# Lightning attention followed by a GELU MLP: a rebuilt prologue, an undecayed state and a last tile in two parts

## The chip, the cores and the metric

One core of one Trainium2 chip runs the whole kernel. The metric is the device time of one execution, in microseconds (us). The kernel before was timed three times: 237.8 us median, 237.49 to 241.02.

## The reference

Block-wise linear attention with a decay per head, then a two-layer MLP with a GELU. Batch 4, 8 heads, 768 positions, head size 64, blocks of 64; the MLP goes from 512 to 2048 and back, over 3072 tokens.

```python
Dmask = np.where(rel >= 0, lam[:, None, None] ** rel[None, :, :], 0.0)
...
for b in range(nb):
    intra = np.einsum('bhic,bhjc->bhij', qb, kb) * Dmask[None]
    intra = np.einsum('bhij,bhjd->bhid', intra, vb)
    inter = np.einsum('bhid,bhde->bhie', qb * lam_pow[None], kv_state)
    out[:, :, sl] = intra + inter
    kb_dec = kb * rev_pow[None]
    kv_state = lam_block[None, :, None, None] * kv_state + np.einsum('bhsd,bhse->bhde', kb_dec, vb)
...
h = x @ w_in
g = 0.5 * h * (1.0 + np.tanh(c * (h + 0.044715 * h * h * h)))
return (g @ w_out).astype(np.float32)
```

## The kernel before, in words

The kernel works in blocks of 128 positions, two of them (index c) to a superblock of 256 (`SB`). There are 24 steps; step s takes one superblock of one batch and one half of the heads (four heads, two pairs `hp` of two heads `hl`). Three superblocks make a sequence, so every six steps the state starts anew.

The decay is put on q and v: q is multiplied by lam to the power of a position (`dq`), v by the reciprocal (`dv`), and the scores are then only masked with ones and zeros (`mask`). Between blocks of 128 the state is multiplied by lam to the power 128.

A step goes through these functions:

- `load_step` (L60) issues three DMAs of 256 KB on the SyncE queue, for q, k and v. `load_win` and `load_wout` (L76, L82) bring the weights in eight pieces of 1 MB into a ring of four buffers (`wst`), `cast_win` and `cast_wout` (L88, L100) turn them into 16 bits: the first piece of w_in on ScalarE, the other three on VectorE, w_out on GpSimd.
- `prep` (L164) makes 16-bit q, k, v: q times `dq` on VectorE (L177), k on ScalarE (L178), v times `dv` on GpSimd (L179).
- `stage_t` (L184) transposes q and k on TensorE into one PSUM tile `Tps` (eight 128x128 transposes, L190) and copies it to `qkT` (L193, VectorE).
- `region(n, s)` (L205) issues for step n the scores `Sps` (16 matmuls, L223), the state's increment K into a part of the tile `OK` (L234), and the masking of the scores to `PT` on VectorE (L240); and for the step s before it the output matmuls (L255) and those with the state (L265), which ScalarE copies to `xT` (L272). There is one buffer each of `Tps`, `Sps` and `OK`.
- `update(n, c)` (L279) adds K to the state on VectorE (`t`, L292 and L294), and GpSimd multiplies the sum with lam^128 twice: into `u` for the next addition (L299) and, head by head, into the block-diagonal 16-bit `ubd` that TensorE uses as weights (L302, two instructions). `t` of the next block reads `u`.

The MLP of a group of superblocks is cut into pieces of work in a list, `filler`: `mm1` (first layer and GELU on ScalarE) and `mm2` (a quarter of a 128-token output tile; after the fourth quarter VectorE copies the tile to `o32` and SyncE writes it with two DMAs, L343 and L345). `fill(n)` takes n pieces from that list. The order of all instructions is the program's order on each engine (`pin`), written out by hand: steps 0 to 3 first (the prologue, L374 to L391), then the weights' casts and `fill(19)`, steps 4 to 7 with their own `fill` counts (L398 to L423), and a loop for the rest. TensorE, VectorE, ScalarE, GpSimd and SyncE each go through their own part of that order without overtaking.

The constants are made at the start, mostly on GpSimd (L126 to L159): `dq` by a power of 16 columns (L132), a power of 8 columns for lam^128 (L149), and eight cleared `ubd` tiles (L159).

Of the kernel before, what the change touches and what calls it, by code (L numbers as in the profile page):

```python
# [15 lines left out]
def kernel(  # L16
# [10 lines left out]
    nc = tc.nc  # L27
# [105 lines left out]
    dv = const.tile([P, H, 2], FP32)
    nc.vector.reciprocal(dv[:], dq[:])
    ident = const.tile([P, P], FP16)
    make_identity(nc, ident)
# [4 lines left out]
    nc.gpsimd.tensor_scalar(rel[64:128], rel[64:128], 128.0, None, ALU.add)  # L141
    mask = const.tile([P, 2 * P], FP32)
    nc.vector.tensor_scalar(mask[:], rel[:].rearrange("p a b c -> p (a b c)"), 0.0, None,
                            ALU.is_ge)

    p128 = const.tile([P, H], FP32)
    nc.gpsimd.memset(p128[:], 128.0)
    lam128 = const.tile([P, H], FP32)
    nc.gpsimd.tensor_tensor(lam128[:], lam_bc[:], p128[:], ALU.pow)  # L149
    lamu = const.tile([P, H // 2], FP32)  # L150
    l3 = lam128[:].rearrange("p (hp two) -> p hp two", two=2)
    nc.gpsimd.tensor_copy(out=lamu[0:64, :], in_=l3[0:64, :, 0])
    nc.gpsimd.tensor_copy(out=lamu[64:128, :], in_=l3[64:128, :, 1])

    ubd = [[const.tile([P, 2, P], FP16, name=f"ubd_{hf}_{i}", tag=f"ubd_{hf}_{i}")
            for i in range(4)] for hf in range(2)]
# [39 lines left out]
    PTs = {}  # L196
# [5 lines left out]
    def half64(i):  # L202
        return slice(64 * i, 64 * i + 64)

    def region(n, s):  # L205
# [54 lines left out]
        for c in range(2):  # L260
            u = ins[c]
            if u is None:
                continue
            for hp in range(2):
                pin(nc.tensor.matmul(OK[:, c, hp * P : hp * P + P], u[:, hp, :],  # L265
                                     o[:, 0, hp, :, half64(c)], start=False, stop=True,
                                     skip_group_check=True))
        g, i = group_of[sbg]
# [5 lines left out]
                                 func=AF.Copy))  # L274

    ins_of = {}
    turn = [0, 0]

    def update(s, c):  # L279

        sbg, half = divmod(s, 2)
        sb = sbg % NSB
        if c == 0:
            ins_of[s] = [state[half][1] if sb > 0 else None, None]
        if c == 1 and sb == NSB - 1:
# [9 lines left out]
        lu = lamu[:, 2 * half : 2 * half + 2].unsqueeze(2).to_broadcast([P, 2, D])  # L295
        bd = ubd[half][turn[half] % 4]
        turn[half] += 1
        uc = ucp.tile([P, 2, D], FP32, tag=f"u{half}", name=f"u_{s}_{c}")
# [13 lines left out]
    def queue_group(g):  # L312
# [158 lines left out]
```

## Time and profile before

| | us |
|---|---|
| median of three runs | 237.8 |
| the profiled execution | 237.57 |
| its span in the trace | 235.7 |
| TensorE busy (share of the span) | 208.0 (88%) |
| VectorE busy | 95.5 (41%) |
| ScalarE busy | 89.0 (38%) |
| GpSimd busy | 93.5 (40%) |
| bytes moved by DMA | 33.89 MB |

The span runs from the first to the last event of the trace; 1.87 us of the profiled execution lie outside it. PE is TensorE, PEld its weight loads, DVE VectorE, ACT ScalarE, POOL GpSimd, SP SyncE; a trailing q is an engine's issuing queue. Times inside the trace are us from the span's start.

### The profile page before, as it was taken

To read this page: it belongs to the slowest core of one execution; us is meant where nothing else is said; L and a number is where in the kernel's file an instruction comes from. 1 tells how busy PE (TensorE), PEld (TensorE's weight loads), DVE (VectorE), ACT (ScalarE), POOL (GpSimd) and SP (SyncE) were. 2 spreads that over 40 slices of the span, in tenths; PEclk is the share of its full clock that TensorE was granted. 3 is DMA by queue.
4 is the path that set the end of the run, shared out by engine and by line. 5 is a ranking of instruction groups with operands and counts; after the bars stand their busy time and mean duration, and the time that the engine had idled before them with its cause. 6 is when DMAs were issued, how large, how long until landed. Compare 5 with 4: busy or idle time off the path is not lost.

```text
span 235.7 us, 5205 instructions
## 1 busy us (share of the span) xinstructions
PE 208.0 (88%) x2192; PEld 113.1 (48%) x2192; DVE 95.5 (41%) x144; ACT 89.0 (38%) x150; POOL 93.5 (40%) x175
## 2 busy tenths in 40 slices
PE   0237599969779999999999999999999999999992
PEld 0126334435458668554545545454554544444440
DVE  0448661045667673564434534335452332100121
ACT  2204376601226417326751137621157610267000
POOL 4989885317277453353254133235325110000000
PEclk9999999999999999999999999999999999999997
DMA  5999789999637058329802739303720012300223
GB/s 150 290 351 386 240 258 323 335 292 273 141 99 218 3 155 238 104 45 243 204 3 45 190 91 302 90 0 70 204 45 0 3 41 51 76 13 3 44 56 79
DMA packets 46247, 33.89 MB, mean 144 GB/s; under 512 B 2192, under 2 KB 39056, under 8 KB 46224
## 3 DMA queue, kind: packets, MB, share of 16 engines
q1 hardware_dynamic: 46080, 33.56, 53.0%
q8 instruction: 17, 0.28, 0.5%
q14 instruction: 6, 0.05, 0.1%
q10 hardware_dynamic: 144, 0.00, 0.0%
HBM read 27.27 MB, written 6.29 MB: 142 GB/s over the span
## 4 chain that ended last, share of the span: by engine, by line
PE 87%; POOL 5%; DVE 3%; ACT 2%; issue 2%; POOLq 0%
PE Hps L324 36%; PE O2ps L335 35%; PE Tps L190 4%; PE Sps L223 4%; PE OK L265 3%; PE OK L255 3%; PE OK L234 1%; POOL dq L132 1%; POOL lam L149 1%; DVE q L177 1%; ACT w_in L92 1%; POOL ubd L159 1%; DVE o L343 1%; ACT xT L272 1%; DVE qkT L193 1%
## 5 line engine op out<-in xcount | busy, mean ns | idle before, releaser
L324 PE MATMUL Hps<-xT,w_in 128*128 128x512 f16 (+1 forms) x448 | 88.0, 352 | 0.0
L335 PE MATMUL O2ps<-w_out,gT 128*128 128x512 f16 x384 | 86.8, 379 | 0.0
L326 ACT ACTIVATE gT<-Hps 128x512 f16<-128x512 f32 x96 | 57.3, 597 | 46.1 <-PE Hps L324 46.1
L324 PEld LDWEIGHTS <-w_in 128*128 128x128 f16 x448 | 43.4, 99 | 37.2 <-issue 1.7
L335 PEld LDWEIGHTS <-gT 128*128 128x128 f16 x384 | 36.6, 98 | 40.2
L299 POOL TENSOR_TENSOR u<-t,lamu 128x128 f32<-128x128 f32 x40 | 17.0, 424 | 89.6 <-DVE t L294 63.0
L272 ACT ACTIVATE xT<-OK 128x512 f16<-128x512 f32 x24 | 14.3, 597 | 73.9 <-PE OK L265 73.9
L343 DVE COPY o<-O2ps 128x512 f32<-128x512 f32 x24 | 16.6, 690 | 54.3 <-PE O2ps L335 54.1
L240 DVE TENSOR_TENSOR PT<-Sps,mask 128x1024 f16<-128x1024 f32 x24 | 29.3, 1221 | 22.8 <-PE Sps L223 22.8
L302 POOL TENSOR_TENSOR ubd<-t,lamu 64x128 f16<-64x128 f32 x80 | 33.5, 418 | 3.0
L193 DVE COPY qkT<-Tps 128x1024 f16<-128x1024 f16 x24 | 16.5, 689 | 36.8 <-PE Tps L190 36.8
L179 POOL TENSOR_TENSOR v<-v,dv 128x512 f16<-128x512 f32 x24 | 25.3, 1055 | 2.2 <-DMA v<-in_v_dram 0.6
L190 PE MATMUL Tps<-ident,q 128*128 128x128 f16 x96 | 10.2, 235 | 14.7 <-DVE q L177 14.7
L177 DVE TENSOR_TENSOR q<-q,dq 128x512 f16<-128x512 f32 x24 | 19.8, 823 | 2.5 <-DMA q<-in_q_dram 2.5
L178 ACT ACTIVATE k<-k 128x512 f16<-128x512 f32 x24 | 14.7, 622 | 7.8 <-DMA k<-in_k_dram 7.8
L190 PEld LDWEIGHTS <-q 128*128 128x128 f16 x96 | 7.5, 105 | 19.3 <-DVE q L177 15.8
L223 PE MATMUL Sps<-qkT 64*64 64x128 f16 x384 | 10.9, 237 | 3.1 <-DVE qkT L193 3.1
L294 DVE TENSOR_TENSOR t<-OK,u 128x128 f32<-128x128 f32 x32 | 9.2, 288 | 9.0 <-POOL u L299 7.0
L255 PE MATMUL OK<-PT,v 64*64 64x128 f16 x384 | 11.1, 233 | 1.9 <-DVE t L294 1.9
L223 PEld LDWEIGHTS <-qkT 64*64 64x64 f16 x384 | 6.7, 114 | 11.8 <-issue 6.1
L234 PE MATMUL OK<-v,k 64*64 64x64 f16 x320 | 7.6, 202 | 3.4 <-POOL v L179 3.0
L103 POOL CAST w_out<-wo 128x1024 f16<-128x1024 f32 x8 | 9.1, 1169 | 3.1 <-DMA wo<-in_moe_w_out_dram 3.1
(29 smaller groups left out, 69.1 us busy)
## 6 DMA issues: line engine op xcount, KB each, us to landing
q<-in_q_dram SPq DMA_DIRECT2D x24, 256.0 KB, 5.4
k<-in_k_dram SPq DMA_DIRECT2D x24, 256.0 KB, 5.3
v<-in_v_dram SPq DMA_DIRECT2D x24, 256.0 KB, 5.2
out_dram<-o SPq DMA_DIRECT2D x48, 128.0 KB, 2.4
wi<-in_moe_w_in_dram SPq DMA_DIRECT2D x4, 1024.0 KB, 10.5
wo<-in_moe_w_out_dram SPq DMA_DIRECT2D x4, 1024.0 KB, 7.8
lam_bc<-in_lam_dram ACTq DMA_DIRECT2D x1, 4.0 KB, 3.6
```

The source lines that it names most:

```text
L177: pin(nc.vector.tensor_tensor(wide(tq), q32[:], decay(dq), ALU.mult))
L179: pin(nc.gpsimd.tensor_tensor(wide(tv), v32[:], decay(dv), ALU.mult))
L190: pin(nc.tensor.transpose(Tps[:, i, hp, j, :], t[:, j, 2 * hp : 2 * hp + 2, :], ident[:]))
L193: pin(nc.vector.tensor_copy(out=o[:], in_=Tps[:]))
L223: pin(nc.tensor.matmul(Sps[half64(c), hl, hp, jk, :], o[half64(hl), 1, hp, jk, half64(c)], o[half64(hl), 0, hp, :, half64(c)], start=True, ...
L240: pin(nc.vector.tensor_tensor(PT[:].rearrange("p a b c d -> p (a b) (c d)"), Sps[:].rearrange("p a b c d -> p (a b) (c d)"), mask[:].unsqu ...
L255: pin(nc.tensor.matmul(OK[half64(hl), c, hp * P : hp * P + P], tv[half64(c), jk, 2 * hp + hl, :], PT[half64(c), hl, hp, jk, :], start=star ...
L302: pin(nc.gpsimd.tensor_tensor(bd[r, :, half64(hl)], t[r], lu[r], ALU.mult))
L324: pin(nc.tensor.matmul(Hps[:, i, :], w_in16[:, c, f * P : (f + 1) * P], x[:, c, :], start=(c == 0), stop=(c == NC - 1)))
L326: pin(nc.scalar.activation(out=gT[:, f0 : f0 + per, :], in_=Hps[:], func=AF.Gelu_apprx_tanh))
L335: pin(nc.tensor.matmul(O2[tau][:], gT[:, f, tau * P : (tau + 1) * P], w_out16[:, f, :], start=(f == 0), stop=(f == NF - 1)))
L343: pin(nc.vector.tensor_copy(out=o32[:], in_=o2[:]))
```

## The change

- lam is loaded first on SyncE's queue, not on ScalarE's. `dq` is a power of 8 columns; its second half is one multiplication by lam, on VectorE. The positions' and the mask's constants are made before lam arrives. lam^128 comes from seven squarings on VectorE, and stands in `lumask`, zero outside the block diagonal, and in `lamu`.
- The eight cleared tiles and the power for lam^128 on GpSimd are gone. `t` is kept undecayed: VectorE forms t = t_before * lam^128 + K (two instructions, one for each head pair), and GpSimd only writes the block-diagonal 16-bit copy, in one instruction of 256 columns.
- Steps 0 to 3 copy their transposes with ScalarE; a one-element GELU at the start loads ScalarE's table.
- The first piece of w_in is cast before `U(2)`; the fourth piece of w_out is loaded ahead of step 5's q, k, v and cast with the third; the `fill` counts of steps 4 to 7 change (36 pieces before the loop, now 39).
- The last 128-token tile is multiplied in two parts, of 384 and 128 columns; each part is copied and written on its own, on two queues.

```diff
-    nc.scalar.dma_start(out=lam_bc[:], in_=lam.unsqueeze(0).to_broadcast([P, H]))
+    pin(nc.sync.dma_start(out=lam_bc[:], in_=lam.unsqueeze(0).to_broadcast([P, H])))
...
-    nc.gpsimd.tensor_tensor(dq[:], lam2, pos[:], ALU.pow)
...
+    pin(nc.scalar.activation(out=warm[:], in_=ident[:, 0:1], func=AF.Gelu_apprx_tanh))
+    dq = const.tile([P, H, 2], FP32)
+    pin(nc.gpsimd.tensor_tensor(dq[:, :, 0], lam_bc[:], pos[:], ALU.pow))
+    sq = [lam_bc] + [const.tile([P, H], FP32, name=f"sq{i}", tag=f"sq{i}") for i in range(7)]
+    for i in range(7):
+        pin(nc.vector.tensor_tensor(sq[i + 1][:], sq[i][:], sq[i][:], ALU.mult))
...
+    pin(nc.vector.tensor_tensor(dq[:, :, 1], dq[:, :, 0], lam_bc[:], ALU.mult))
+    dv = const.tile([P, H, 2], FP32)
+    pin(nc.vector.reciprocal(dv[:], dq[:]))
...
-    for i in range(4):
-        for hf in range(2):
-            nc.gpsimd.memset(ubd[hf][i][:], 0.0)
...
-        pin(nc.vector.tensor_copy(out=o[:], in_=Tps[:]))
+        if s < 4:
+            pin(nc.scalar.activation(out=o[:], in_=Tps[:], func=AF.Copy))
+        else:
+            pin(nc.vector.tensor_copy(out=o[:], in_=Tps[:]))
...
-            pin(nc.vector.tensor_tensor(t[:], K, state[half][0][:], ALU.add))
...
-        pin(nc.gpsimd.tensor_tensor(uc[:], t[:], lu, ALU.mult))
-        for hl in range(2):
-            r = half64(hl)
-            pin(nc.gpsimd.tensor_tensor(bd[r, :, half64(hl)], t[r], lu[r], ALU.mult))
-        state[half] = (uc, bd)
+            for hp in range(2):
+                pin(nc.vector.scalar_tensor_tensor(
+                    t[:, hp, :], state[half][0][:, hp, :],
+                    lamu[:, 2 * half + hp : 2 * half + hp + 1], K[:, hp, :], ALU.mult, ALU.add))
+        bd = ubp.tile([P, 2, 2, D], FP16, tag=f"u{half}", name=f"u_{s}_{c}")
+        pin(nc.gpsimd.tensor_tensor(
+            bd[:], t[:].unsqueeze(2).to_broadcast([P, 2, 2, D]),
+            lumask[:, 2 * half : 2 * half + 2, :].unsqueeze(3).to_broadcast([P, 2, 2, D]),
+            ALU.mult))
+        state[half] = (t, bd)
...
+        def mm2_last(tau):
+            dst = rows(tau)
+            o32 = otp.tile([P, DM], FP32, tag="o32", name="o32")
+            for lo, hi in ((0, 384), (384, DM)):
+                o2 = ps_M.tile([P, hi - lo], FP32, tag="M", name="O2ps")
+                for f in range(NF):
+                    pin(nc.tensor.matmul(o2[:], gT[:, f, tau * P : (tau + 1) * P],
+                                         w_out16[:, f, lo:hi], start=(f == 0),
+                                         stop=(f == NF - 1)))
+                pin(nc.vector.tensor_copy(out=o32[:, lo:hi], in_=o2[:]))
+                for j, eng in ((0, nc.sync), (1, nc.scalar)):
+                    pin(eng.dma_start(out=dst[j][:, lo:hi], in_=o32[half64(j), lo:hi]))
...
     stage_t(3)
+    cast_win(0)
     U(2)
-    cast_win(0)
...
     cast_wout(2)
+    cast_wout(3)
     fill(3)
     R(4, None)
     U(4)
+    fill(6)
     prep(5)
     stage_t(5)
-    cast_wout(3)
-    fill(3)
+    fill(1)
     R(5, 4)
     U(5)
-    fill(3)
+    fill(1)
     prep(6)
     stage_t(6)
     fill(1)
     R(6, 5)
     U(6)
-    fill(3)
+    fill(4)
```

GpSimd from its first constant to step 1's v, before (`dq` and `dv` are the decay factors, `lam` here is lam^128, `ubd` the cleared tiles):

```order
L132 TENSOR_TENSOR dq<-lam_bc,pos 128x16
masks.py:199 AFFINE_SELECT ident<-ident 128x128
L141 TENSOR_SCALAR rel<-rel 64x256
L147 MEMSET p_203 128x8
L159 MEMSET ubd_0_210 128x256
L149 TENSOR_TENSOR lam_205<-lam_bc,p_203 128x8
...
L159 MEMSET ubd_3_217 128x256
L179 TENSOR_TENSOR v_0_228<-v_0_108,dv 128x4x2x64
L179 TENSOR_TENSOR v_1_245<-v_1_114,dv 128x4x2x64
```

The same stretch of GpSimd after the change:

```order
L128 IOTA pos 128x8
L133 IOTA rel 128x256
L130 TENSOR_SCALAR pos<-pos 64x8
masks.py:197 MEMSET ident 128x128
masks.py:199 AFFINE_SELECT ident<-ident 128x128
L149 TENSOR_TENSOR dq<-lam_bc,pos 128x8
L181 TENSOR_TENSOR v_0_231<-v_0_111,dv 128x4x2x64
L181 TENSOR_TENSOR v_1_248<-v_1_117,dv 128x4x2x64
```

Between the power and step 0's v nothing is left; the identity stands ahead of the power now.

VectorE in steps 4 to 6, before (`q_5` and `q_6` are the steps' decayed q, `o` a finished output tile, `t` a state):

```order
L240 TENSOR_TENSOR PT_751<-Sps,mask 128x1024
L294 TENSOR_TENSOR t_0_753<-OK,u_1_473 128x128
L177 TENSOR_TENSOR q_5_759<-q_5_148,dq 128x4x2x64
L193 COPY qkT_774<-Tps 128x1024
L240 TENSOR_TENSOR PT_816<-Sps,mask 128x1024
L294 TENSOR_TENSOR t_0_840<-OK,u_1_546 128x128
L343 COPY o_850<-O2ps 128x512
L343 COPY o_858<-O2ps 128x512
L343 COPY o_866<-O2ps 128x512
L177 TENSOR_TENSOR q_6_870<-q_6_156,dq 128x4x2x64
L193 COPY qkT_885<-Tps 128x1024
```

And after the change:

```order
L245 TENSOR_TENSOR PT_746<-Sps,mask 128x1024
L299 SCALAR_TENSOR_TENSOR t_0_748<-t_1_471,lamu,OK 128x64 x2
L346 COPY o_769<-O2ps 128x512
L346 COPY o_777<-O2ps 128x512
L346 COPY o_785<-O2ps 128x512
L179 TENSOR_TENSOR q_5_789<-q_5_153,dq 128x4x2x64
L198 COPY qkT_804<-Tps 128x1024
L245 TENSOR_TENSOR PT_837<-Sps,mask 128x1024
L299 SCALAR_TENSOR_TENSOR t_0_861<-t_1_538,lamu,OK 128x64 x2
L179 TENSOR_TENSOR q_6_870<-q_6_159,dq 128x4x2x64
L198 COPY qkT_885<-Tps 128x1024
```

The three tile copies stand ahead of step 5's q now, not of step 6's; on TensorE the six pieces of MLP work that they end lie between step 4's scores and step 5's transposes.

ScalarE around steps 11 to 13, before (`xT` is the MLP's input; 1332 is the tile of the group of steps 8 to 11; gT_1717 is that group's first GELU output):

```order
L178 ACTIVATE k_13_1638<-k_13_1365 128x4x2x64
L272 ACTIVATE xT_1332<-OK 128x2x2x128
L178 ACTIVATE k_14_1764<-k_14_1495 128x4x2x64
L326 ACTIVATE gT_1717<-Hps 128x512 x4
L272 ACTIVATE xT_1847<-OK 128x2x2x128
```

And after the change:

```order
L180 ACTIVATE k_13_1634<-k_13_1368 128x4x2x64
L277 ACTIVATE xT_1332<-OK 128x2x2x128
L330 ACTIVATE gT_1712<-Hps 128x512 x3
L180 ACTIVATE k_14_1758<-k_14_1505 128x4x2x64
L330 ACTIVATE gT_1712<-Hps 128x512 x4
```

The group's first GELUs follow its last `xT` directly; on TensorE its first-layer matmuls follow step 11's state matmuls with no older piece of work between them.

## Rows read from the trace of the kernel before

**Rows 1.** Stretches: from:to, length, busy time of PE, PEld, DVE, ACT, POOL, clock, DMA.
```profile
47.20:68.00 20.80, 15.75 (x202) 8.24 (x200) 11.56 (x17) 2.75 (x5) 9.88 (x17) 1.00 0.84 200
100.00:204.00 104.00, 104.00 (x1094) 53.07 (x1093) 42.60 (x67) 41.60 (x71) 33.37 (x70) 1.00 0.38 95
```

**Rows 2.** Timeline of the start: from, us, engine line operation, idle before it, and its releaser.
```profile
4.36 2.92 POOL L132 TENSOR_TENSOR dq<-lam_bc,pos 128x16 f32<-128x16 f32 x1 [2.34 <-DMA lam_bc<-in_lam_dram]
...
7.32 0.25 DVE L134 RECIPROCAL dv<-dq 128x16 f32<-128x16 f32 x1 [7.32 <-POOL dq L132]
...
8.96 0.67 DVE L177 TENSOR_TENSOR q<-q,dq 128x512 f16<-128x512 f32 x1
8.98 2.19 POOL L149 TENSOR_TENSOR lam<-lam_bc,p 128x8 f32<-128x8 f32 x1
...
9.70 0.61 PE L190 MATMUL Tps<-ident,q 128*128 128x128 f16 x4 [9.70 <-DVE q L177]
...
15.14 0.43 PE L234 MATMUL OK<-v,k 64*64 64x64 f16 x16 [2.98 <-POOL v L179]
```

**Rows 3.** Timeline of one turn of the prologue, step 2 to step 3.
```profile
19.82 0.69 DVE L193 COPY qkT<-Tps 128x1024 f16<-128x1024 f16 x1
...
20.57 0.64 PE L223 MATMUL Sps<-qkT 64*64 64x128 f16 x16 [0.79 <-DVE qkT L193]
...
21.86 0.13 PEld L265 LDWEIGHTS <-ubd 128*128 128x128 f16 x2 [0.24 <-POOL ubd L302]
...
22.79 2.17 ACT L92 ACTIVATE w_in<-wi 128x512 f16<-128x512 f32 x4
```

**Rows 4.** Timeline of the prologue's end, step 3 to the first MLP matmuls.
```profile
23.89 0.64 PE L223 MATMUL Sps<-qkT 64*64 64x128 f16 x16 [0.78 <-DVE qkT L193]
...
26.39 0.60 ACT L272 ACTIVATE xT<-OK 128x512 f16<-128x512 f32 x1 [1.43 <-PE OK L265]
...
27.89 0.29 DVE L294 TENSOR_TENSOR t<-OK,u 128x128 f32<-128x128 f32 x1 [0.58 <-POOL u L299]
...
28.24 0.64 PE L255 MATMUL OK<-PT,v 64*64 64x128 f16 x16 [1.88 <-DVE t L294]
...
29.28 15.31 PE L324 MATMUL Hps<-xT,w_in 128*128 128x512 f16 x64
```

**Rows 5.** Timeline of TensorE in steps 4 to 7: the scores, then three waits.
```profile
50.15 0.42 PE L223 MATMUL Sps<-qkT 64*64 64x128 f16 x16
...
52.70 0.40 PE L190 MATMUL Tps<-ident,q 128*128 128x128 f16 x4 [2.01 <-DVE q L177]
...
60.98 0.40 PE L190 MATMUL Tps<-ident,q 128*128 128x128 f16 x4 [1.47 <-DVE q L177]
...
67.66 0.40 PE L190 MATMUL Tps<-ident,q 128*128 128x128 f16 x4 [1.58 <-DVE q L177]
```

**Rows 6.** Timeline of the end, and DMA issues: count, KB each, median us to landing.
```profile
231.20 0.69 DVE L343 COPY o<-O2ps 128x512 f32<-128x512 f32 x1 [2.76 <-PE O2ps L335]
231.92 1.11 SPq L345 DMA_DIRECT2D out_dram<-o  x2
...
out_dram<-o SPq DMA_DIRECT2D x48, 128.0 KB, 2.4
...
lam_bc<-in_lam_dram ACTq DMA_DIRECT2D x1, 4.0 KB, 3.6
```

**Rows 7.** Groups by line and form: count | busy us, mean ns | idle before, releaser.
```profile
L179 POOL TENSOR_TENSOR v<-v,dv 128x512 f16<-128x512 f32 x24 | 25.3, 1055 | 2.2 <-DMA v<-in_v_dram 0.6
L299 POOL TENSOR_TENSOR u<-t,lamu 128x128 f32<-128x128 f32 x40 | 17.0, 424 | 89.6 <-DVE t L294 63.0 <-DVE t L292 25.4
...
L294 DVE TENSOR_TENSOR t<-OK,u 128x128 f32<-128x128 f32 x32 | 9.2, 288 | 9.0 <-POOL u L299 7.0 <-ACT xT L272 1.2
```

**Rows 8.** The tile of w_in's pieces: its DMA issues (ns, first and last start), and landing.
```profile
L78 SPq DMA_DIRECT2D wi<-in_moe_w_in_dram x4: 832/832/833, 10.6 to 13.2; - x4
...
DMA to landing us min/median/max: 7.2/10.5/13.6
```

More of the change, by code (lines that the diff above doesn't have):

```diff
@@ L47 @@
     ptp = ctx.enter_context(tc.tile_pool(name="ptp", bufs=3))
-    ucp = ctx.enter_context(tc.tile_pool(name="ucp", bufs=4))
+    ucp = ctx.enter_context(tc.tile_pool(name="ucp", bufs=3))
+    ubp = ctx.enter_context(tc.tile_pool(name="ubp", bufs=4))
     xtp = ctx.enter_context(tc.tile_pool(name="xtp", bufs=3))
@@ L115 @@
     load_wout(2)
+    load_wout(3)
     load_step(5)
-    load_wout(3)
     for s in range(6, 11):
@@ L123, in load_ahead @@
             load_step(s)
-    pos = const.tile([P, H, 2], FP32)
-    nc.gpsimd.iota(pos[:], pattern=[[0, H], [1, 2]], base=-63, channel_multiplier=2,
+    pos = const.tile([P, H], FP32)
+    nc.gpsimd.iota(pos[:], pattern=[[0, H]], base=-63, channel_multiplier=2,
                    allow_small_or_imprecise_dtypes=True)
     nc.gpsimd.tensor_scalar(pos[64:128], pos[64:128], 128.0, None, ALU.subtract)
-    lam2 = lam_bc[:].unsqueeze(2).to_broadcast([P, H, 2])
-    dq = const.tile([P, H, 2], FP32)
-    nc.gpsimd.tensor_tensor(dq[:], lam2, pos[:], ALU.pow)
[L133 to L136, printed above, removed]
     rel = const.tile([P, 2, 2, 64], FP32)
@@ L140 @@
                    allow_small_or_imprecise_dtypes=True)
-    nc.gpsimd.tensor_scalar(rel[64:128], rel[64:128], 128.0, None, ALU.add)
+    ident = const.tile([P, P], FP16)
+    make_identity(nc, ident)
     mask = const.tile([P, 2 * P], FP32)
[L143 to L149, printed above, removed]
-    lamu = const.tile([P, H // 2], FP32)
[L151 to L156, printed above, removed]
-    for i in range(4):
-        for hf in range(2):
-            nc.gpsimd.memset(ubd[hf][i][:], 0.0)
+    for hl in range(2):
+        r = slice(64 * hl, 64 * hl + 64)
+        pin(nc.vector.tensor_scalar(mask[r], rel[r].rearrange("p a b c -> p (a b c)"),
+                                    -128.0 * hl, None, ALU.is_ge))
+    lumask = const.tile([P, H // 2, 2], FP32)
+    pin(nc.vector.memset(lumask[:], 0.0))
+    warm = const.tile([P, 1], FP16)
+    pin(nc.scalar.activation(out=warm[:], in_=ident[:, 0:1], func=AF.Gelu_apprx_tanh))
[4 more added lines that the diff above has]
+        pin(nc.vector.tensor_tensor(sq[i + 1][:], sq[i][:], sq[i][:], ALU.mult))
+    l3 = sq[7][:].rearrange("p (hp two) -> p hp two", two=2)
+    for hl in range(2):
+        r = slice(64 * hl, 64 * hl + 64)
+        pin(nc.vector.tensor_copy(out=lumask[r, :, hl], in_=l3[r, :, hl]))
+    lamu = const.tile([P, H // 2], FP32)
+    pin(nc.vector.tensor_tensor(lamu[:], lumask[:, :, 0], lumask[:, :, 1], ALU.add))
+    pin(nc.vector.tensor_tensor(dq[:, :, 1], dq[:, :, 0], lam_bc[:], ALU.mult))
+    dv = const.tile([P, H, 2], FP32)
+    pin(nc.vector.reciprocal(dv[:], dq[:]))
     a16 = {}
@@ L264, in region @@
             for hp in range(2):
-                pin(nc.tensor.matmul(OK[:, c, hp * P : hp * P + P], u[:, hp, :],
+                pin(nc.tensor.matmul(OK[:, c, hp * P : hp * P + P], u[:, hp].rearrange("p l d -> p (l d)"),
                                      o[:, 0, hp, :, half64(c)], start=False, stop=True,
@@ L276 @@
     ins_of = {}
-    turn = [0, 0]
     def update(s, c):
@@ L293, in update @@
         else:
-            pin(nc.vector.tensor_tensor(t[:], K, state[half][0][:], ALU.add))
[L295 to L298, printed above, removed]
-        pin(nc.gpsimd.tensor_tensor(uc[:], t[:], lu, ALU.mult))
-        for hl in range(2):
-            r = half64(hl)
-            pin(nc.gpsimd.tensor_tensor(bd[r, :, half64(hl)], t[r], lu[r], ALU.mult))
-        state[half] = (uc, bd)
+            for hp in range(2):
[8 more added lines that the diff above has]
+        state[half] = (t, bd)
         if c == 0:
@@ L345, in mm2, with rows @@
                 pin(nc.sync.dma_start(out=dst[j], in_=o32[half64(j), :]))
+        def rows(tau):
+            row0 = groups[g][0] * SB + tau * P
+            return out[row0 : row0 + P, :].rearrange("(p j) e -> j p e", j=2)
+        def mm2_last(tau):
+            dst = rows(tau)
+            o32 = otp.tile([P, DM], FP32, tag="o32", name="o32")
[8 more added lines that the diff above has]
+                    pin(eng.dma_start(out=dst[j][:, lo:hi], in_=o32[half64(j), lo:hi]))
         for f in range(0, NF, per):
@@ L353, in queue_group @@
             order = [(tau, part) for tau in range(NTAU) for part in range(4)]
+        if g == len(groups) - 1:
+            order = order[:-4]
         for tau, part in order:
             filler.append(lambda tau=tau, part=part: mm2(tau, part))
+        if g == len(groups) - 1:
+            filler.append(lambda: mm2_last(NTAU - 1))
     def fill(n):
```

2 lines of the change are left out of this document (removed).

## The prediction

> **What bounds the kernel now.** I read the stretches first. From 100 to 204 us TensorE is busy for 104.00 of 104.00 us, while no other engine reaches half [rows 1]; all attention steps of the loop and all MLP work run there back to back, at a granted clock of 1.00, and no edit to another engine can be felt as long as this stays so. The time is therefore the sum of three things outside it: how late TensorE gets its first MLP matmul, how long it still waits in steps 4 to 7 (5.05 of 20.80 us between 47.2 and 68.0 are idle [rows 1]), and what follows its last matmul. The timeline of the start shows the first transposes at 9.70, held by step 0's q, and that step's K matmuls at 15.14, after 2.98 us of waiting for GpSimd's v [rows 2]. A turn of the prologue is 3.3 us (scores at 20.57 and 23.89 [rows 3, 4]), each opened by the copy of the transposes. At its end a chain through xT, two state additions and a GpSimd product between them holds TensorE for 1.88 us, and the MLP starts at 29.28 [rows 4]. Steps 5, 6 and 7 then wait 2.01, 1.47 and 1.58 us for their q [rows 5]; these 5.06 us are all the idle time of that stretch. The end is a copy of 0.69 us and two DMA issues [rows 6].
>
> **The start.** The power of 16 columns takes 2.92 us, the one of 8 columns 2.19 [rows 2]. lam arrives at 4.36 [rows 2], and I leave it there, since its DMA is issued first on either queue. Before, q0's product began at 8.96, because reciprocal and mask had to come after the power. Now: 4.36 + 2.19 = 6.55, the second half of `dq` and the reciprocal at no more than 0.25 each (the reciprocal's row) with handoffs, so q0 from 7.2 to 7.9 and the transposes from 7.9: 1.8 earlier than 9.70. On VectorE ten small instructions for lam^128 stand ahead of this; lam is there at 4.36, so they are hidden by the power as long as each takes under 0.22. The nearest row, the reciprocal with 16 columns, is 0.25 and would make them 0.3 us late; a floor is nothing. I take them as hidden, since eight columns and a plain product should stay under it.
> The Trainium skill (VectorE: DVE Perf Modes, Side-by-side: where the cycles go) gives each VectorE instruction about 150 cycles of set-up at 0.96 GHz, so about 1.6 us for ten, an estimate by that page; by it they end at 6.0 and cost nothing, by the reciprocal's row they cost 0.3. No run here shows a product of 8 columns.
>
> The copy of the transposes moves from VectorE (0.69 [rows 3]) to ScalarE. No ScalarE row has 1024 columns: four of 512 take 2.17 back to back [rows 3], so each further one adds 0.52 to the first one's 0.62, and 1024 columns can't take more than 1.14; below, 0.69 as on VectorE. I take 1.10, near the two. That is 0.41 dearer in each of the four copies, and each is on the path, because scores start only behind it.
> The Trainium skill (ScalarE: Activation LUTs, What ACT_TABLE_LOAD costs) gives 186 ns + 0.833 ns per column, 1.04 us for 1024; by it the four copies would be 0.24 us cheaper together than in my sum. Its 0.61 for 512 columns agrees with our 0.62, but no run here shows 1024.
>
> So step 0's scores come at 7.9 + 1.05 (eight transposes; four take 0.61 [rows 2]) + 1.10 and handoffs = 10.1, its K matmuls some 0.45 behind at 10.55 (the scores' 0.64 holds their drain), with no wait: v0 takes 1.05 [rows 7] from the reciprocal at 7.2, because the second power, the copies and the cleared tiles no longer stand ahead of it on GpSimd. Against 15.14 that is 4.6 gained.
>
> **The turns and the prologue's end.** From step 0's K matmuls to step 3's scores it was 23.89 - 15.14 = 8.75. Three dearer copies add 1.2; the short wait for `ubd` in two of the turns (0.24 [rows 3]) goes, since GpSimd's share per state falls from three instructions to one, priced between the 128 columns' 0.42 and the 512 columns' 1.06, about 0.63 on a line between them [rows 7]. So step 3's scores are at 10.55 + 8.75 + 1.2 - 0.4 = 20.1. Then a new order decides: w_in's first casts (2.17) stand on ScalarE ahead of xT of step 2, from 20.05 to 22.2, so xT ends at 22.85. Behind it are step 3's two state additions. A pair of 64-column instructions costs between 0.29 (one of 128 columns, rows 7) and 0.58; I take 0.40, so 23.3 and 23.7, without the 0.58 wait for GpSimd between them [rows 4]. Output and state matmuls follow, 1.04 as before (28.24 to 29.28): first MLP matmul at 24.8. **The prologue gains 4.5.** What is behind it keeps up: w_in's pieces 2 to 4 are landed by 13.2 + 13.6 = 26.8 at the latest [rows 8], and their casts on VectorE begin at 23.7, ahead of an MLP that needs 15.31/16, about a microsecond, for 128 columns of w_in [rows 4]. The fourth piece of w_out passes step 5's three loads on SyncE; both are earlier by the prologue's gain, so they are not late.
>
> **Steps 4 to 7.** Step 5's transposes now stand behind six pieces of MLP work, but its q behind the copy of the last of them: just the arrangement that step 6 had, so 1.47 [rows 5]. Step 6 has one piece (four matmuls at 15.31/64 [rows 4], 0.95) between the scores and its transposes. Before, step 5 with none showed 52.70 - 50.15 = 2.55 from scores to transposes [rows 5]; now xT of step 4 and two additions come between too, some 0.3, so 2.85, less 0.54 of scores and K matmuls (2.55 - 2.01), some 0.4 of output and state matmuls (1.04 in the prologue, where matmuls run at about half the loop's pace) and 0.95 of the piece: 1.0. Step 7 has four pieces, 3.5 us or more, under which q is ready: none. The waits fall from 5.06 to 2.5: **2.5 gained.** With only half of it (q later by a copy in either step) 1.5, at best 3.6.
>
> **The loop.** Three more pieces are spent ahead of it. At step 12 the list is then empty when its next group is queued, so that group's first matmuls wait for xT (0.60 [rows 4] plus handoffs, less two matmuls that need only the other half): **0.4 lost**, none to 0.6. Later groups keep one piece as cover.
>
> **The end.** The last copy has 128 columns, 0.29 like a state addition [rows 7] in place of 0.69. The second issue no longer stands behind the first, 0.47 of the 1.11 [rows 6]. **0.9 gained**, if ScalarE's DMA lands like SyncE's; its only one of before took 3.6 against 2.4 [rows 6], which would make it 0.3 lost.
>
> **Sum.** -4.5 - 2.5 + 0.4 - 0.9 = -7.5, from the profiled execution's own 237.57 (0.2 under the median of the runs): **230.1 us**. The GpSimd time saved in the loop counts nothing: TensorE does not wait there.
>
> **Rivals.** (a) *The turn of the prologue grows into its own bound.* If the ScalarE copy is at 1.14, a pair of state instructions at 0.58 and the small products late, the prologue's gain loses 0.2 + 0.6 + 0.3, and ScalarE's queue behind k's loads up to another 0.5; with the half gain in steps 4 to 7 and a tail without gain the sum is -2.9 - 1.5 + 0.6 = -3.8: 233.8, within 2%. For it: ScalarE is in series with TensorE in each turn now. Against: VectorE is relieved of four copies.
> (b) *The copy costs what VectorE's did.* Four copies at 0.69 gain 1.6 more, steps 4 to 7 lose only half their remaining wait: 227.3. Against: ScalarE's own rows.
> (c) *Slower: w_in's casts block ScalarE.* They now stand ahead of xT; if the first piece of w_in were not there at 20.05, each us of it delays xT, the state, and the first MLP matmul by one. It was issued at 10.6 and landed 7.2 later at the earliest of the four [rows 8], 17.8, with 0.4 for lam's place on SyncE 18.2. It would have to come after 27.6 to eat all of 7.5; at 30 it gives 232.5 + 7.5 = 240. Only a lam broadcast that holds up the queue could do it.
> (d) *The change doesn't act:* the MLP starts earlier but waits for w_out behind an unchanged stream of loads. w_out's pieces need buffers that the casts free, so they move with the casts; if they did not, only the 2.5 and the end would be left: 234.6.
>
> **Chances.** The forecast 0.72, (a) 0.10, (b) 0.10, (c) 0.03, (d) 0.05. Best of all bounds is 226.7, worst without (c) 234; leaving a tenth on either side, 227.6 to 233.2. What can be told from no change is about 2%, 4.8 us: the forecast, (b) and a little of (a) are faster, most of (a) and (d) within, (c) slower: 0.86, 0.11, 0.03.
>
> **What would show it.** Right: first transposes near 7.9, no wait of step 0's K matmuls for v, ScalarE's copies near 1.1, first MLP matmul near 24.8, waits for q of about 1.5, 1.0 and 0 in steps 5 to 7, a wait of TensorE for xT near step 12 only, and about 3.3 us from the last copy to the end of the span. Wrong: a first MLP matmul after 27, a ScalarE wait for w_in's DMA, TensorE idle for a DMA between 45 and 60, or idle time anywhere in the loop beyond step 12.

## The result, and the profile after

| | before | after |
|---|---|---|
| median, us | 238.63 (4 runs) | 229.8 (4 runs, 229.57 to 230.02) |
| profiled execution, us | 237.57 | 230.02 |
| its span, us | 235.7 | 228.1 |
| ratio of the runs, after to before | | 0.9617, 95% interval 0.9536 to 0.9698 |

The change makes the kernel 3.8% faster; 230.1 us were forecast. The sum is right to 0.3 us, but not each of its terms: the prologue gave more than was priced, steps 4 to 7 less, and one cost was not in the sum. That these cancel is luck. The forecast was counted from an execution of 237.57 us; of 27 later executions of the kernel before, 21 took 239.4 to 241.0 us at a mean granted clock of 0.992 or 0.993, and six took 237.5 to 238.3 at 0.995 or more, so the medians above differ by 8.8 us where the two traces differ by 7.6.

The start after the change, from the timeline (from, us, engine line operation, idle before and its releaser):

```profile
3.74 0.17 DVE L152 TENSOR_TENSOR sq<-lam_bc 128x8 f32<-128x8 f32 x1 [1.71 <-DMA lam_bc<-in_lam_dram]
3.79 1.67 POOL L149 TENSOR_TENSOR dq<-lam_bc,pos 128x8 f32<-128x8 f32 x1 [1.36 <-DMA lam_bc<-in_lam_dram]
...
5.60 0.16 DVE L159 TENSOR_TENSOR dq<-dq,lam_bc 128x8 f32<-128x8 f32 x1
...
5.96 0.63 DVE L179 TENSOR_TENSOR q<-q,dq 128x512 f16<-128x512 f32 x1
6.65 0.61 PE L192 MATMUL Tps<-ident,q 128*128 128x128 f16 x4 [6.65 <-DVE q L179]
...
6.99 1.04 POOL L181 TENSOR_TENSOR v<-v,dv 128x512 f16<-128x512 f32 x1 [1.53 <-DMA v<-in_v_dram]
...
9.23 0.43 PE L239 MATMUL OK<-v,k 64*64 64x64 f16 x16
```

Against [rows 2], lam is there 0.57 us earlier, the power of 8 columns takes 1.67 us instead of the 2.19 of the other power of 8 columns, and the transposes start at 6.65 instead of 9.70. The K matmuls of step 0 stand at 9.23 without a wait, where they waited 2.98 us for v until 15.14. v0 itself now waits for its DMA, no longer for GpSimd.

The last turn of the prologue and its end, from the same timeline, against [rows 3, 4]:

```profile
15.32 0.64 PE L228 MATMUL Sps<-qkT 64*64 64x128 f16 x16 [1.11 <-ACT qkT L196]
...
17.82 1.02 ACT L196 ACTIVATE qkT<-Tps 128x1024 f16<-128x1024 f16 x1 [0.26 <-PE Tps L192]
...
18.74 2.17 ACT L93 ACTIVATE w_in<-wi 128x512 f16<-128x512 f32 x4
18.90 0.64 PE L228 MATMUL Sps<-qkT 64*64 64x128 f16 x16 [1.11 <-ACT qkT L196]
...
20.82 0.58 ACT L277 ACTIVATE xT<-OK 128x512 f16<-128x512 f32 x1
...
21.44 0.85 DVE L299 SCALAR_TENSOR_TENSOR t<-t,lamu,OK 128x64 f32<-128x64 f32 x4 [0.62 <-ACT xT L277]
...
22.35 0.64 PE L260 MATMUL OK<-PT,v 64*64 64x128 f16 x16 [1.62 <-DVE t L299]
...
23.32 6.93 PE L328 MATMUL Hps<-xT,w_in 128*128 128x512 f16 x23
```

A turn is longer than before, 3.58 us (15.32 to 18.90) against 3.3, because of the ScalarE copy; the MLP starts at 23.32 against 29.28 all the same. Four state instructions go back to back in 0.85 with no GpSimd between them.

What TensorE waits for from 26 us to the end (engine line waited for: us in all, times, longest):

```profile
PE Tps L192 <- DVE q L179: 2.4, 2, 1.4
PE Tps L192 <- ACT k L180: 1.0, 1, 1.0
PE Hps L328 <- ACT xT L277: 0.3, 1, 0.3
```

The waits of [rows 5] were 5.06; here are 2.4 for q in steps 5 and 6, a new one of 1.0 for step 7's k, and the small one near step 12. The timeline shows why k is late:

```profile
61.39 0.60 ACT L330 ACTIVATE gT<-Hps 128x512 f16<-128x512 f32 x1 [0.28 <-PE Hps L328]
...
62.26 0.60 ACT L330 ACTIVATE gT<-Hps 128x512 f16<-128x512 f32 x1 [0.28 <-PE Hps L328]
...
62.76 1.14 ACT L180 ACTIVATE k<-k 128x512 f16<-128x512 f32 x2
...
63.43 0.40 PE L192 MATMUL Tps<-ident,k 128*128 128x128 f16 x4 [0.98 <-ACT k L180]
```

Step 7's k is queued on ScalarE behind three GELUs, each of which waits for the MLP matmuls that now stand ahead of the transposes. The end of the trace, to be read beside [rows 6]:

```profile
224.28 1.11 SPq L365 DMA_DIRECT2D out_dram<-o  x2
224.28 1.38 ACTq L365 DMA_DIRECT2D out_dram<-o  x2
224.58 0.29 DVE L363 COPY o<-O2ps 128x128 f32<-128x128 f32 x1 [0.33 <-PE O2ps L360]
```

From the last copy's start to the end of the span it was 235.7 - 231.2 = 4.5, and is 228.1 - 224.58 = 3.5.

The difference of the spans, 7.6, is split up here by the chains of the two traces. Such a chain is the work that ended last, followed back to what released it; on it a matmul counts from the end of the one before, so the first MLP matmul stands at 23.53 where the timeline has 23.32. The first MLP matmuls on the chain start at 23.53 instead of 29.49, -5.96; the 64 of them take 15.57 instead of 15.10, +0.47; the waits of steps 4 to 7 are 3.36 instead of 5.06, -1.70; step 12 +0.25; the end -0.98; the last tile in two parts 3.51 instead of 3.45, +0.06. Together -7.86, 0.26 more than the spans differ. Some 0.16 of that stand behind step 12's wait, where ten matmuls take 2.32 on the chain and 2.16 at the loop's pace; the rest is not traced.

### The profile page after: what moved, and what is told of

It reads as the page before. It is cut to its first block, busy times and chain, and to the rows that moved or that the text cites. A ratio compares the mean times of both kernels' runs of the same rounds, so it can differ in the third digit from the quotient of the medians.

```text
span 228.1 us, 5197 instructions
## 1 busy us (share of the span) xinstructions
PE 208.2 (91%) x2208; PEld 114.3 (50%) x2208; DVE 97.4 (43%) x186; ACT 92.1 (40%) x154; POOL 62.2 (27%) x82
## 4 chain that ended last, share of the span: by engine, by line
PE 90%; ACT 4%; DVE 3%; DMA 1%; issue 1%; DVEq 0%; ACTq 0%
PE Hps L328 37%; PE O2ps L339 34%; PE Tps L192 6%; PE Sps L228 4%; PE OK L270 3%; PE OK L260 3%; ACT qkT L196 2%; PE O2ps L360 2%; DMA lam_bc<-in_lam_dram 1%; PE OK L239 1%; ACT w_in L93 1%; DVE q L179 1%; ACT xT L277 1%; DVE t L299 1%; DVE sq L152 1%
## 5 line engine op out<-in xcount | busy, mean ns | idle before, releaser
L328 PE MATMUL Hps<-xT,w_in 128*128 128x512 f16 (+1 forms) x448 | 89.1, 353 | 0.3 <-ACT xT L277 0.3
L339 PE MATMUL O2ps<-w_out,gT 128*128 128x512 f16 x368 | 84.0, 379 | 0.0
L303 POOL TENSOR_TENSOR u<-t,lumask 128x256 f16<-128x256 f32 x40 | 25.8, 653 | 113.4 <-DVE t L299 83.4
L339 PEld LDWEIGHTS <-gT 128*128 128x128 f16 x368 | 35.1, 98 | 38.0
L198 DVE COPY qkT<-Tps 128x1024 f16<-128x1024 f16 x20 | 13.8, 692 | 41.7 <-PE Tps L192 41.7
L346 DVE COPY o<-O2ps 128x512 f32<-128x512 f32 x23 | 15.8, 688 | 32.8 <-PE O2ps L339 32.8
L179 DVE TENSOR_TENSOR q<-q,dq 128x512 f16<-128x512 f32 x24 | 17.1, 714 | 6.6 <-DMA q<-in_q_dram 6.6
L299 DVE SCALAR_TENSOR_TENSOR t<-t,lamu,OK 128x64 f32<-128x64 f32 x64 | 14.5, 276 | 2.5 <-ACT xT L277 1.0
L192 PE MATMUL Tps<-ident,k 128*128 128x128 f16 x96 | 10.3, 235 | 1.0 <-ACT k L180 1.0
L270 PE MATMUL OK<-qkT,u 128*128 128x128 f16 x80 | 9.3, 235 | 0.0
```

The costliest lines, as they stand in the source:

```text
L179: pin(nc.vector.tensor_tensor(wide(tq), q32[:], decay(dq), ALU.mult))
L299: pin(nc.vector.scalar_tensor_tensor(t[:, hp, :], state[half][0][:, hp, :], lamu[:, 2 * half + hp : 2 * half + hp + 1], K[:, hp, :], ALU.m ...
L303: pin(nc.gpsimd.tensor_tensor(bd[:], t[:].unsqueeze(2).to_broadcast([P, 2, 2, D]), lumask[:, 2 * half : 2 * half + 2, :].unsqueeze(3).to_b ...
L328: pin(nc.tensor.matmul(Hps[:, i, :], w_in16[:, c, f * P : (f + 1) * P], x[:, c, :], start=(c == 0), stop=(c == NC - 1)))
```

## The experiments

All are the changed kernel (229.57 to 230.02 us) with one thing different, except where two are named; "first MLP matmul" is its row in the timeline, 23.32 in the changed kernel, unless the chain is named (23.53). "The 64 matmuls" are the first layer's first 64, 15.57 on the changed kernel's chain.

**Copies of steps 0 to 3 by VectorE.**

```diff
-        if s < 4:
-            pin(nc.scalar.activation(out=o[:], in_=Tps[:], func=AF.Copy))
-        else:
-            pin(nc.vector.tensor_copy(out=o[:], in_=Tps[:]))
+        pin(nc.vector.tensor_copy(out=o[:], in_=Tps[:]))
```

> The changed kernel with one part undone: the transposes of steps 0 to 3 are copied by VectorE again. Theory (the ScalarE copy of 1.02 us stands on the path in each turn, 0.33 us dearer than VectorE's 0.69): the turn shrinks from 3.58 us to about 3.3, the first MLP matmul comes about 1.0 us earlier than 23.3, total about 229.0 us. Rival 1 (VectorE, with 2.9 us of work in a turn already, becomes the bound of the turn with 0.69 more): the turn stays at 3.6 or grows, first MLP matmul at 23.3 or later, total 229.8 to 230.5.

Three executions took 230.03 to 230.67 us; the traced one took 754 us, with TensorE busy for 98% of it, and says nothing of the others. The same kernel again:

> The first experiment's kernel once more (steps 0 to 3 copied by VectorE), since its trace was of an execution three times as long. Theory of the ScalarE copy on the path: turn about 3.3 us, first MLP matmul 1.0 us earlier than 23.3, 229.0 us. Rival of VectorE as the turn's bound, which the first times (230.0 to 230.7) speak for: copies wait on VectorE behind its additions, turn 3.6 or more, 229.8 to 230.5 us.

230.73 to 231.19 us. Each theory had a half: the turn shrinks, and the first MLP matmul stays. The timeline:

```profile
14.51 0.64 PE L225 MATMUL Sps<-qkT 64*64 64x128 f16 x16 [0.78 <-DVE qkT L195]
...
17.96 0.64 PE L225 MATMUL Sps<-qkT 64*64 64x128 f16 x16 [0.94 <-DVE qkT L195]
...
18.78 2.19 ACT L93 ACTIVATE w_in<-wi 128x512 f16<-128x512 f32 x4 [1.97 <-DMA wi<-in_moe_w_in_dram]
...
22.39 0.64 PE L257 MATMUL OK<-PT,v 64*64 64x128 f16 x16 [2.56 <-DVE t L296]
...
23.36 1.91 PE L325 MATMUL Hps<-xT,w_in 128*128 128x512 f16 x4
```

The copies are indeed 0.33 dearer on ScalarE and on the path: the turn is 3.45 instead of 3.58, and step 3's scores come at 17.96 instead of 18.90. But nothing of it arrives: ScalarE now stands 1.97 us before w_in's first piece, which lands at 18.78, just when the changed kernel's ScalarE came to it of itself (18.74). xT is queued behind these casts, so the first MLP matmul is at 23.36 as before. The ScalarE copy costs nothing only because the prologue has another floor, the landing of w_in. The total is even 1.3 us higher; in the traces the 64 matmuls take 16.31 instead of 15.57, and the waits for q in steps 5 and 6 are 2.8 instead of 2.4.

**Old piece counts in steps 4 to 7.** `fill(3)`, `fill(3)`, `fill(3)`, `fill(1)`, `fill(3)`, and the last w_out cast behind `stage_t(5)`, as before the change.

> The changed kernel with the piece counts of steps 4 to 7 and the place of the last w_out cast as before (36 pieces ahead of the loop). Theory: the three waits for q of 2.0, 1.5 and 1.6 us (5.1 in all) come back in place of 1.4 + 1.0 for q and 1.0 for step 7's k, and the 0.3 us wait for xT near step 12 goes: 1.4 us slower, 231.2 us. Rival (these waits are set by DMA landings, which did not move): the waits stay at about 3.4 and the total at 229.8.

231.37 us median (230.29 to 232.82). TensorE's waits for q are 5.0 us again (11.7 in all, less the 6.7 ahead of the first transposes):

```profile
PE Tps L192 <- DVE q L179: 11.7, 4, 6.7
```

The waits for k and near step 12 are gone. By these waits the new counts are worth 1.4 us (5.0 against 3.4 and 0.25), as the theory said. The median's 1.6 does not show that by itself. The traced execution, 230.29 us, is only 0.3 slower than the traced one of the changed kernel, because its 64 matmuls take 14.77. And two of the four executions, 232.12 and 232.82, had a mean granted clock of 0.993, like most of the kernel before, where the two others had 0.997 and 1.000 and the changed kernel's four 0.999 or 1.000. So the old counts seem to cost TensorE's clock in some executions as well; no trace shows such an execution, so where the clock fell stays open.

**The removed GpSimd work put back.**

```diff
+    pin(nc.gpsimd.memset(p128[:], 128.0))
...
+    pin(nc.gpsimd.tensor_tensor(lam128[:], lam_bc[:], p128[:], ALU.pow))
...
+    for i in range(8):
+        pin(nc.gpsimd.memset(idle[i][:], 0.0))
```

> The changed kernel with the removed GpSimd work put back ahead of step 0's v, its results unused: the power of 8 columns by 128 and eight cleared tiles. Theory (GpSimd's queue ahead of v0 held the first K matmuls): v0 starts near 9.9 instead of 6.99, the K matmuls of step 0 wait until about 11.0 instead of 9.23, first MLP matmul 1.8 us later, total 231.6. Rival (slack of the later turns takes it up, and the start's gain came from the earlier transposes alone): the total moves by less than 0.5.

230.79 us median (230.15 to 231.58); timeline:

```profile
5.71 1.65 POOL L153 TENSOR_TENSOR lam<-lam_bc,p 128x8 f32<-128x8 f32 x1
...
7.31 2.07 POOL L156 MEMSET idle<- 128x256 f16 x8
...
9.35 2.04 POOL L188 TENSOR_TENSOR v<-v,dv 128x512 f16<-128x512 f32 x2
10.44 0.43 PE L246 MATMUL OK<-v,k 64*64 64x64 f16 x16 [0.82 <-POOL v L188]
```

The wait for v is back, 0.82 us. The first MLP matmul on the chain is at 24.74 instead of 23.53, 1.2 later, and the median rose by 1.0. The mechanism holds, at two thirds of its price, because power and clearing took 3.8 us here, from 5.53 to 9.35, where 4.4 were expected.

**The decayed state on GpSimd.**

```diff
+            pin(nc.vector.tensor_tensor(t[:], K, state[half][0][:], ALU.add))
...
+        pin(nc.gpsimd.tensor_tensor(uc[:], t[:], lu, ALU.mult))
```

> The changed kernel with the decayed state back: GpSimd multiplies t into a second tile, VectorE only adds; the single block-diagonal write stays. Theory (the state's hop over GpSimd is on the path only at the prologue's end, where one addition waits for the other): first MLP matmul 0.3 to 0.6 us later, turns unchanged, no wait in the loop, total 230.2 to 230.4. Rival (GpSimd's load of 17 us more matters along the loop): TensorE waits in the loop and the total rises by over 2 us.

230.0 us median (229.55 to 231.12). The additions' wait at the prologue's end is 1.9 instead of 1.6, the first MLP matmul on the chain at 23.77 instead of 23.53, and there is no new wait in the loop. So the undecayed state is worth some 0.2 us, and the GpSimd time saved along the loop nothing.

**The last tile whole.**

```diff
-        if g == len(groups) - 1:
-            order = order[:-4]
...
-            filler.append(lambda: mm2_last(NTAU - 1))
```

> The changed kernel with the last 128-token tile whole again: one copy of 512 columns and two writes one behind the other on SyncE. Theory (0.4 us of copy and 0.5 to 0.6 us of a second issue stand behind the last matmul): from the last matmul's end to the span's end 4.5 us instead of 3.5, total 0.9 to 1.0 us slower, 230.7 us. Rival (landing and the program's end set the tail, and two queues give no more than one): under 0.3 us slower.

230.83 us median (230.66 to 231.8), 1.0 more; the last copy starts at 225.26 in a span of 229.8, 4.5 us from its end. That is the theory's price, to a tenth. (The traced execution, 231.8 us, also has 16.24 for the 64 matmuls.)

**Earlier q, k, v of steps 5 to 7.**

```diff
     U(4)
+    prep(5)
     fill(6)
-    prep(5)
     stage_t(5)
+    prep(6)
     fill(1)
     R(5, 4)
     U(5)
     fill(1)
-    prep(6)
     stage_t(6)
...
     U(6)
+    prep(7)
     fill(4)
-    prep(7)
     stage_t(7)
```

> The changed kernel with q, k and v of steps 5, 6 and 7 prepared one place earlier: step 5's ahead of the six pieces, step 6's ahead of step 5's scores, step 7's ahead of the four pieces. Theory (the three waits of TensorE, 1.4 and 1.0 us for q behind output copies and state additions on VectorE, 1.0 us for step 7's k behind three GELUs on ScalarE, are queue order alone): all three go, 3.3 us faster, 226.5 us. Rival (the loads of steps 5 to 7 arrive too late for that, or VectorE's earlier q delays the scores' masking): waits of 1.5 us or more remain.

225.79 us median (225.23 to 226.22), 4.0 less. From 26 us on only this is left of TensorE's waits:

```profile
PE Hps L328 <- ACT xT L277: 0.3, 1, 0.3
```

All three were queue order. They cost more than the 3.36 us listed: eight transposes take 0.62 on the chain where TensorE waited for them, 0.45 where it did not, and 3.36 + 3 x 0.17 = 3.87 answers to the spans' 228.1 - 224.3 = 3.8, of which the 64 matmuls (15.46) make 0.1.

**Unread work that keeps TensorE busy in the prologue.** `warm_pe(n)` issues n matmuls of 512 columns whose result nobody reads.

```diff
     prep(0)
+    warm_pe(9)
     stage_t(0)
+    warm_pe(2)
...
     stage_t(1)
+    warm_pe(2)
...
     U(3)
+    warm_pe(3)
     R(None, 3)
```

> The changed kernel with TensorE work added whose result nobody reads: nine matmuls of 512 columns ahead of the first transposes, two behind each step's transposes, three ahead of the last output matmuls of the prologue. Theory (TensorE's matmuls take double their loop time in the whole prologue and in the first eight or so MLP matmuls because it idles a third of that time; kept busy it takes its full pace there): eight transposes take 0.62 instead of 1.05 us, the turn falls from 3.58 to 2.6 to 3.0, the 64 first-layer matmuls take 13.9 instead of 15.6, total 3 to 5 us less, 225 to 227 us. Rival (the pace does not answer to this work): turns stay at 3.6 and the total at 229.8 to 230.3.

229.88 us median (228.65 to 230.29), nothing gained; the trace shows the gain and where it went:

```profile
13.46 0.42 PE L228 MATMUL Sps<-qkT 64*64 64x128 f16 x16 [0.68 <-ACT qkT L196]
...
16.05 0.42 PE L228 MATMUL Sps<-qkT 64*64 64x128 f16 x16 [0.68 <-ACT qkT L196]
...
18.35 2.19 ACT L93 ACTIVATE w_in<-wi 128x512 f16<-128x512 f32 x4 [2.35 <-DMA wi<-in_moe_w_in_dram]
...
21.96 0.64 PE L260 MATMUL OK<-PT,v 64*64 64x128 f16 x16 [2.95 <-DVE t L299]
```

The pace answers: a turn is 2.6 us (13.46 to 16.05), the scores 0.42 instead of 0.64. But ScalarE waits 2.35 us for w_in at 18.35, xT behind it, and TensorE 2.95 us behind that. The first MLP matmul on the chain comes at 23.14, only 0.39 earlier, and the 64 matmuls take 15.99, 0.42 more. The stretches (from:to, length, busy times of PE, PEld, DVE, ACT, POOL, granted clock, DMA) then show the clock fall:

```profile
9.00:20.00 11.00, 7.01 (x197) 4.32 (x185) 8.31 (x16) 6.99 (x12) 7.46 (x9) 1.00 1.11 345
20.00:23.00 3.00, 1.04 (x21) 0.87 (x22) 1.95 (x6) 1.02 (x3) 1.40 (x2) 0.60 1.05 384
23.00:26.00 3.00, 3.00 (x10) 1.04 (x8) 2.08 (x3) 1.20 (x2) 0.23 (x1) 0.50 1.05 386
```

0.50 of 2.4 GHz is the 1.2 GHz level, and the first MLP matmuls ran there.

**lam on ScalarE's queue.** `nc.scalar.dma_start` in place of `nc.sync.dma_start`.

> The changed kernel with lam loaded from ScalarE's queue again, beside SyncE's loads. Theory (lam arrived 0.6 us earlier because it is first on the one queue that the loads use): the power starts near 4.36 again instead of 3.79, the first transposes near 7.2 instead of 6.65. Rival (a difference between executions): the power starts at 3.8.

One execution, 231.11 us. Landing of lam, and the power, from the list of its tile (ns, first and last start):

```profile
L149 POOL TENSOR_TENSOR dq<-lam_bc,pos x1: 1665/1665/1665, 5.1 to 5.1; 128x8 f32<-128x8 f32 x1
...
DMA to landing us min/median/max: 4.3/4.3/4.3
```

In the changed kernel the power starts at 3.8 after a landing of 3.0, so the queue matters, even more than expected: 1.3 us here, against 0.57 between before and after. Every other trace of these experiments, with lam first on SyncE, has a landing of 2.9 to 3.1. The first MLP matmul on the chain is at 24.82, 1.29 later: nothing takes it up.

**Both, with w_in's casts behind the last xT.** The earlier preparation and the unread work (four more matmuls ahead of the MLP) together, and:

```diff
     stage_t(3)
-    cast_win(0)
     U(2)
...
     R(None, 3)
+    cast_win(0)
+    warm_pe(4)
```

> The changed kernel with the earlier q, k and v of steps 5 to 7, the unread TensorE work of the warm run (four more such matmuls behind the prologue's last state matmuls), and w_in's first casts behind the last xT on ScalarE. Theory (in the warm run ScalarE stood 2.35 us for w_in's DMA with xT behind it, which gave back the faster turns and slowed TensorE again): without the cast ahead of xT the first MLP matmul comes near 20.4, its 64 first-layer matmuls take about 14 us, and with 4.0 us from the earlier preparation the total is 220 to 222 us. Rival (the MLP then waits for casts and landings of w_in's other pieces instead): the 64 matmuls take 16 us or more with waits, total 224 to 226.

223.21 us median (222.82 to 224.11), 0.9308 of the kernel before (0.925 to 0.9367), the fastest with the next. The 64 matmuls take 14.30, but start at 22.53, not at 20.4:

```profile
17.77 0.30 PE L260 MATMUL OK<-PT,v 64*64 64x128 f16 x7 [1.11 <-issue]
...
18.44 0.60 ACT L277 ACTIVATE xT<-OK 128x512 f16<-128x512 f32 x1 [2.55 <-PE OK L270]
...
21.56 2.18 ACT L93 ACTIVATE w_in<-wi 128x512 f16<-128x512 f32 x4
...
22.53 13.65 PE L328 MATMUL Hps<-xT,w_in 128*128 128x512 f16 x60
```

TensorE stops for 1.11 us in the middle of 16 matmuls, for nothing that the profile shows; the run with the unread work alone has such a stop, 0.95, at the same place. What it is stays open. It is half of the 2.1 us by which the MLP is late. For the rest, the chain goes through the four added matmuls behind the last state matmuls: 1.71 us from 21.03 on, at a granted clock of 0.53 between 20 and 23. Without them w_in's first cast, which begins at 21.56 and takes 0.62, would have let the MLP start near 22.2 at the earliest, an estimate.

**The same with VectorE's copies.**

> The combined kernel with VectorE making the copies of steps 0 to 3. Theory (at full pace of TensorE a turn of 2.6 us is less than VectorE's 2.9 to 3.6 us of work with the copy): turns grow to over 3 us, first MLP matmul later by 1 us or more than in the combined kernel. Rival (a copy of 0.69 instead of 1.02 shortens the turn): earlier by 0.5 to 1 us.

223.26 us median (222.91 to 223.6): no difference. The last turn is 3.10 us (scores at 13.96 and 17.06) where the combined kernel has 2.60, as the theory said, but its microsecond did not come: the stop in the 16 matmuls is 0.40 here instead of 1.11, and the first MLP matmul, at 22.56, waits for w_in's first cast, which begins at 21.89.

**The casts' place without the unread work.** The earlier preparation, and `cast_win(0)` behind `R(None, 3)`.

> The kernel of the earlier preparation with w_in's first casts behind the last xT on ScalarE, and no unread TensorE work. Theory (at TensorE's slow pace the scores come just as w_in's first piece lands, so the casts ahead of xT cost it only about 0.1 us, and behind the last xT they keep the first MLP matmul waiting for a first cast of 0.6 us): first MLP matmul 0.5 to 1.5 us later than 23.3, total 226.3 to 227.3 us. Rival (the casts' place alone brought the combined kernel's 2.6 us): total 223 to 224.5.

227.41 to 228.07 us in three executions (a fourth took 318.85), some 2 us more than with the casts ahead:

```profile
24.62 3.59 PE L328 MATMUL Hps<-xT,w_in 128*128 128x512 f16 x8 [1.21 <-ACT w_in L93]
```

The MLP waits 1.21 us for the first cast, as the theory said; the rest above its range is that the 64 matmuls took 16.33 in this trace, 0.87 more than with the casts ahead. So the casts' place does not bring the combined kernel's gain: alone it loses 2 us. That it pays once TensorE's faster pace has brought xT ahead of w_in's landing follows only from adding up (the unread work alone gains nothing, the earlier preparation 4.0, the combined kernel 6.6); both together with the casts ahead were not run.

## Why the prediction was right, point by point

- **The first transposes** were put at 7.9 and came at 6.65. Two terms failed here. "lam arrives at 4.36, and I leave it there, since its DMA is issued first on either queue" is wrong: on SyncE's queue it came at 3.8, and with the queue alone put back at 5.1. And the power took 1.67, not the 2.19 of the row of the other power; put back behind it in the experiment, that other power took 1.65 too, so 2.19 was not a property of eight columns. Why it was longer in the kernel before was not tried.
- **The ten small instructions** run from 3.74 to 5.68, 1.94 us; the power ends at 5.46, so they are hidden but for the 0.14 by which the second half of `dq` comes later. The estimate from the Trainium skill (VectorE: DVE Perf Modes, Side-by-side: where the cycles go) put them at 1.6 together; measured they start 0.20 apart with 0.17 busy, between that estimate and the reciprocal's 0.25.
- **The ScalarE copy** was put at 1.10 and takes 1.02; the 1.04 worked out from the Trainium skill (ScalarE: Activation LUTs, What ACT_TABLE_LOAD costs), an estimate, was nearer than the bound from rows. That it stands on the path of each turn is shown by the turn of 3.3 to 3.5 with VectorE's copy.
- **The prologue** gained 5.96 where 4.5 was forecast; the start's 1.25 and the copies' 0.3 are about that difference. v's wait went as told, and came back with the GpSimd work. Of the 5.96, lam's queue, the GpSimd work and the undecayed state, each undone alone, take back 1.29, 1.2 and 0.2; the narrower power, the order of mask and reciprocal and the casts' old place were not undone alone, and what they bring is read from the timelines only. The casts ahead of xT were seen as the new order that decides, and rival (c) had the right place: the changed kernel comes to w_in's casts at the moment its first piece lands, and the two prologues that were faster than this with the casts ahead of xT waited there. It was given a landing of 18.2; in the changed kernel it was 18.6 (issued at 10.7, 7.9 to landing), in those two 18.8 and 18.4.
- **Not in the sum:** the first 64 MLP matmuls. 15.57 against 15.10 is what TensorE's slow pace at the MLP's start cost more; with an unchanged prologue the experiments gave 14.77 to 16.24, so a term of this size is the spread from trace to trace and need not be the change's.
- **Steps 4 to 7:** "Step 7 has four pieces, 3.5 us or more, under which q is ready: none" failed. q was ready; k was not, behind three GELUs on ScalarE, and TensorE waited 0.98. The prediction looked at one of the two queues that the transposes wait for. Steps 5 and 6 were right, 1.39 and 0.99 against 1.47 and 1.0. Gained 1.7, not 2.5.
- **Step 12 and the end:** 0.25 of 0.4, and 0.98 of 0.9; ScalarE's two writes landed in 2.5 and 2.2, SyncE's two of the same sizes in 2.1 and 2.0: not quite alike, but far from the 3.6 that was feared.
- **GpSimd in the loop** was worth nothing, as told: the decayed state brought no wait there.

## What to carry to other kernels

When a step is moved, go through every queue that its parts enter: q, k and v of one step were prepared on three engines, and looking at q alone missed k behind the GELUs. A prologue can have several floors at once; undoing one suspected cost then moves nothing, and only the row that says what is waited for now tells that the cost was real. The best version here holds, beside the earlier preparation, which brings 4.0 us alone, two changes that bring nothing or lose 2 us alone: the unread work and the later casts.

## What the runs showed of the hardware that was not expected

The pace of matmuls is not always what the clock column says. In the changed kernel its mean over the span is 1.000, while weight loads of the first MLP matmuls, which follow the matmuls one to one, start 0.43 us apart until 26.74 and half as far apart from 27.07 on:

```profile
26.31 0.15 PEld L328 LDWEIGHTS <-w_in 128*128 128x128 f16 x1 [0.27 <-issue]
26.74 0.15 PEld L328 LDWEIGHTS <-w_in 128*128 128x128 f16 x1 [0.28 <-issue]
27.07 4.85 PEld L328 LDWEIGHTS <-w_in 128*128 128x128 f16 x23 [0.18 <-issue]
```

512 columns in 0.43 us are the 1.2 GHz level, 23 loads in 4.85 us (0.21 each) that of 2.4 GHz. In the warm run, where TensorE had reached the faster level before it fell back, the column does show the fall, 0.60 and 0.50. From 23 to 26 us the loads of the first MLP matmuls are 0.43 apart in both kernels, and the column says 0.50 in the warm run's row above and 1.00 in the changed kernel's (here TensorE's busy time, clock and DMA):

```profile
23.00:26.00 3.00, 3.00 (x11) 1.00 1.05 388
```

The traced execution of 754 us goes further: 16 matmuls of 512 columns take 13.13 us on its chain, 0.82 each, again with 1.00 in the column.

The chain has the 64 matmuls of the same prologue (the old piece counts change only what follows) once at 15.57 and once, here, at 14.77:

```profile
23.59 14.77 PE Hps L328 x64
```

Four traces have this same prologue. The faster spacing of the loads begins in them at 25.47 (this one), 26.74, 27.07 and 28.44, and the 64 matmuls take 14.77, 15.46, 15.57 and 16.24. So the moment at which the pace doubles moves by 3 us between traces and the time by 1.5, which is as much as several of these experiments are worth.

A load of 4 KB landed 3.0 us after its issue as the first on the loads' own queue, and 3.6 and 4.3 us from another engine's queue beside them.
